# Unit 3 of a fused attention and gated layer kernel: activated in chunks in PSUM and projected by seven products, with the weight sums made two steps earlier

## The chip, the cores and the metric

The kernel runs on one core of a Trainium2 chip. The metric is the device time of one execution in microseconds (us), from repeated runs. All arithmetic is in 32-bit floats.

## The reference

Two stages follow each other. The first is a linear attention with a decaying state, over 4 batches, 8 heads, 768 tokens and a head width of 48:

```python
for t in range(S):
    cur = u * k[t] v[t]^T
    y[t] = r[t] (state + cur)
    state = w[t] * state + k[t] v[t]^T      # w between 0.8 and 0.95
```

The heads of a token are joined to a row of 384 values, which gives 3072 rows `x`. The second stage is a gated layer with 2048 hidden columns:

```python
h = x @ w_in                     # 384 -> 2048
g = h * erf(softplus(h))
out = g @ w_out                  # 2048 -> 384
```

## The kernel before

**Units and steps.** A unit is two batches times 128 tokens, 256 rows in all; there are 12 units, one for each step s of 0 to 11. Step s computes the attention of unit s (`attend` for steps 0 to 4, `attend_late` for 5 to 11) and passes its rows on as `xT`. Beside it, TensorE computes the hidden layer of unit s-1 and the projection of unit s-3. So unit 3 has its hidden layer in step 4, and is projected in step 6. `attend` and `attend_late` issue attention work; between, tokens are worked off that issue pieces of the other two.

**The hidden layer** (`hidden`) comes in 8 pieces (token H). One is 12 TensorE instructions (L775) into one of the two PSUM buffers "m" and a ScalarE copy of 512 columns to SBUF (L784). The buffer is free for the piece after next when that copy is done. Each unit has two halves of hidden columns, g = 0 and 1, each a tile `h` of 8 by 256.

**Activation, two ways.** Where the unit is below `FAST`, `activate` puts three stages on the list `later`, for each half: Softplus of all 2048 columns into the SBUF tile `room` (L757), Erf in place (L760), and two VectorE products h times room (L764). Token A takes stages from that list. From unit `FAST` on, a unit is activated in four chunks of 1024 columns: token s is a Softplus into the first slot of `room` (L731), token e is an Erf from there into a PSUM lane (L735; "ey" into the banks of y, "ep" into the buffer pp1), and token m is VectorE's product of h and that lane (L740). Each change between Softplus and Erf brings a table load on ScalarE.

**Projection, two ways.** `project` (L807) uses 32 products of 128 rows with 384 columns, each of them two TensorE instructions. It comes in 8 pieces (token P); the sixth and the eighth end with a ScalarE copy "o" of 128x384 out of the "m" buffers (L816), and the output is sent. `project_fast` (L883) takes seven block products of 192 columns (the scheme of Strassen and Winograd on 2x2 blocks), 7 pieces of 16 TensorE instructions. For it:

- four sums of weights are formed once, by `mix_weights`: t3, t2 and t4 into the tile `mixed`, and t1 in the place of the upper right block of w_out. This last one destroys a block that `project` needs. Tokens T (VectorE) and G (GpSimd) send one such sum each (L831).
- four sums of activations per unit, S1 to S4, are formed on VectorE by `blend` (L860 to L866), from quarters of h. Tokens k11p, k22y and so on first copy a quarter to a PSUM lane on ScalarE (`to_lane`, L843): the digits name the quarter, the letter the lane (p for pp1, y for the banks of y).

**Order.** All engines run in program order, written out by hand. In steps 0 to 3 the tables STAGES and CONVERT say what goes where; step 3 is `DIRECT - 1`. In step 4 (`DIRECT`) `in_order` does so; from step 5 on the strings LATE and USUAL, seven stages per step ("front", "near", 0 to 4). Token F goes on with `prepare(s + 1)`, which scales r and k for the next step on VectorE (L263), sums products over the heads (L367), with part of the products on GpSimd (L377, L381), and at last forms the tile `own` (L426).

**In `attend_late`,** the order is: products of level 5 (L452), stages front and near, the product kT times spread (L597), stage 0, products of the last level with two copies `own` and one `few` by ScalarE (L471, L557), stage 1, the state products into PSUM (L538), stage 2, the two `middle` adds (L615), stage 3, the new state (L622), stage 4. The next step opens with `from_own(.., 1)` (L486), a small VectorE copy, and level 5 of its own (L452), which waits for the scaling in the last F of the step before.

Of the kernel before, what the change touches and what calls it, by code (L numbers as in the profile page):

```python
# [15 lines left out]
ALU = mybir.AluOpType  # L16

P = 128
FAST = 4
EP = 64  # L20
HC = 64
NC = 2
# [17 lines left out]
DIRECT = 4  # L40
# [21 lines left out]
def kernel(  # L62
# [14 lines left out]
    nc = tc.nc  # L77
    PSUM = bass.MemoryType.PSUM

    n_steps, _, _, JP, C = rkw.shape  # L80
# [4 lines left out]
    _, NT, DM = w_out.shape  # L85
# [45 lines left out]
    def products(shape, n=None):  # L131


        if n is not None:
            return ps_p.tile(shape, FP32, name=f"pp{n}")
        n = 0 if turns["converting"] else turns["next"]
        turns["next"] = 1 - n
        return ps_p.tile(shape, FP32, name=f"pp{n}")
# [31 lines left out]
    def near_log(s):  # L170
        return NEAR_LOG - (s == DIRECT)
# [85 lines left out]
    def scale(s, level):  # L257

        in_t, tots = loaded[s][0], ready[s][1]
        half, nb = 1 << (level - 1), JP * C >> level  # L260
        n = 1 if s > DIRECT and level == LOG else 2
        halves = view(in_t[:, 0:2], half, [[JP * C - half, n], [2 * half, nb], [1, half]])
        nc.vector.tensor_mul(  # L263
            halves, halves, view(tots[level - 1], 0, [[1, n], [2, nb], [0, half]])
        )
# [170 lines left out]
    def parts_of(s):  # L436

        c, i = divmod(s, SPC)
        in_t, vt = loaded[s]
        made, tots, tot = ready[s]  # L440
        ends = tot.rearrange("p (n h) -> p n h", h=NC)
        return c, in_t, vt, made, states[i][c % 2], states[i][1 - c % 2], ends

    def level_products(pp, rk, level):

        half = 1 << (level - 1)
        m = HC if level <= MASKED else half
        for n in range(JP):
            for s0 in range(0, C, HC):
                for e in range(NE):  # L450
                    t0 = s0 if level <= MASKED else s0 + half
                    nc.tensor.matmul(  # L452
                        pp[s0 : s0 + m, e, n, :m],
                        lhsT=rk[rows(e), 1, n, s0 : s0 + m],
                        rhs=rk[rows(e), 0, n, t0 : t0 + m],
                        start=True,
                        stop=True,
                    )
# [166 lines left out]
    def attend(s, xT, place, behind):  # L625

        c, in_t, vt, made, S, S_next, ends = parts_of(s)
        K = in_t[:, 1]
        RK = in_t[:, 0:2]


        following = prepare(s + 1) if s + 1 < n_steps else iter(())
        own = made if s >= DIRECT else att.tile([P, NH, HC], FP32, name="own")

        def keep_busy(*columns):
            zeros = states[1][0][:].rearrange("p n d -> p (n d)")
            for n in columns if not s else ():
                nc.tensor.matmul(
                    y[:].rearrange("p e j q t -> p (e j q t)")[:, :n], lhsT=ident[:],
                    rhs=zeros[:, :n], start=True, stop=True, skip_group_check=True,  # L640
                )

        def stay_warm(times=1, where=None):
            for _ in range(times):
                ps = where or ps_m.tile([P, NP * C], FP32, name="m")
                nc.tensor.matmul(
                    ps[:], lhsT=ident[:], rhs=ws[s][:, :NP], start=True, stop=True
                )

        if s == DIRECT:  # L650
            next(following)
        for level in range(near_log(s) + 1 if s == DIRECT else 1, LOG + 1):
            rk = made[:] if level == 1 else RK
            pp = products([P, NE, JP, HC])
            level_products(pp, rk, level)
            if level == LOG and s == DIRECT:
                spread_blocks(s + 1, pp)
            scale(s, level)
            keep_busy(DM, DM // 2)
            if level == 1 and s == 1:  # L660
                stay_warm()
            if s == 1 and level == 2:
                behind(None)
            got = pp[:].rearrange("p e n t -> p (e n) t")
            if level == 1:
                if not s:
                    nc.vector.tensor_copy(out=first[:], in_=mask_sb[:, 0, :])
                nc.vector.tensor_mul(
                    own[:], got, first[:, None, :].to_broadcast([P, NH, HC])
                )  # L670
            else:
                take_level(own, pp, level)
            if level > 1 and (s, level) != (DIRECT, LOG - 1):
                next(following, None)
            place(level - 1)

        from_own(s, own, 1)
        ps = products([P, JP, P])
        for n in range(JP):
            nc.tensor.transpose(ps[:, n, :], K[:, n, :], ident[:])  # L680
        if not s:
            stay_warm()
        kT = att.tile([P, NH, D], FP32, name="kT", bufs=1)
        nc.scalar.copy(
            kT[:].rearrange("p (e n) d -> p e n d", e=NE),
            ps[:].rearrange("p n (e d) -> p e n d", e=NE)[..., :D],
        )
        if c:
            nc.gpsimd.tensor_mul(
                faded[0][:], S[:], ends[:, :, 0:1].to_broadcast([P, JP, D])  # L690
            )
        next(following, None)
        place(LOG)


        if s:

            ps = products([P, NC, JP, HC], 1 if s == 1 else None)
            ps = [ps[:, h] for h in range(NC)]
        else:  # L700
            ps = [ps_m.tile([P, JP, HC], FP32, name="m") for h in range(NC)]
        state_part(s, kT, ps)
        from_own(s, own, 0)
        if not s:
            stay_warm(1, products([P, NP * C]))
        for e in range(NE):
            if c:
                nc.vector.tensor_add(middle[rows(e)], faded[0][rows(e)], ps[0][rows(e), :, :D])
            else:
                nc.vector.tensor_copy(middle[rows(e)], ps[0][rows(e), :, :D])  # L710
        nc.gpsimd.tensor_mul(faded[1][:], middle[:], ends[:, :, 1:2].to_broadcast([P, JP, D]))
        for e in range(NE):
            nc.vector.tensor_add(S_next[rows(e)], faded[1][rows(e)], ps[1][rows(e), :, :D])
        for _ in following:
            pass
        place(LOG + 1)
        through_state(s, xT)
        behind()
# [23 lines left out]
    def hidden(of, xT, gs, cut):  # L742
# [25 lines left out]
        for g in range(NG):  # L768
            h = hid.tile([P, FG, UNIT], FP32, name="h")
            gs.append(h)  # L770
            for f in range(0, FG, FT):
# [12 lines left out]
                nc.scalar.copy(h[:, f : f + FT, :], ps[:])  # L784
                if of >= FAST:
                    if f % (2 * FT):
# [145 lines left out]
    def piece(kind, of):  # L932
        if not 0 <= of < n_steps:
            return
        if of not in kind:
            if kind is hids:
                kind[of] = hidden(of, xTs[of], gated[of], not of)
            else:
                kind[of] = (project_fast if of >= FAST else project)(of, gated[of])
        next(kind[of])  # L940

    def in_order(s, k):
# [3 lines left out]
        for what in order[k]:  # L946
# [8 lines left out]
    STAGES_LATE = ("front", "near", 0, 1, 2, 3, 4)  # L955
    LATE = {
        DIRECT + 1: (
            "", "", "A P P P A P P", "F F F A P P P", "T", "H H F", "A s H H H F G ep H H H"
        ),
        DIRECT + 2: (  # L960
            "s P", "m", "ey P m s P P ep P m P", "s P P F ey m k22p k11y F F", "S1",
            "S2 S3 H k12p S4 H F", "s H ey m H H F G G s H ep H H",
        ),
        n_steps - 1: (
            "s P", "m", "ey P m s P P ep P", "m P P", "S", "H H", "s H ey m H H s H ep H H"
# [7 lines left out]
    def run_late(s, tokens, following=None):  # L973

        for what in tokens.split():
            if what == "A":
                advance()
            elif what == "P":
                piece(projs, s - 3)
            elif what == "H":  # L980
                piece(hids, s - 1)
            elif what == "F":
                next(following, None)
            elif what in ("T", "G"):
                mixing.send(nc.vector if what == "T" else nc.gpsimd)
            elif what == "s":
                softplus_chunk()
            elif what[0] == "e":
                erf_chunk(what[1])
            elif what == "m":  # L990
                multiply_chunk()
            elif what[0] == "k":
                to_lane(s - 2, what[1:3], what[3])
            else:
                blend(s - 2, *(int(n) for n in what[1:]))
                if what == "S3":
                    del lanes["11"], lanes["22"]
                elif what == "S4":
                    del lanes["12"]
# [15 lines left out]
    mixing = mix_weights()  # L1015
# [6 lines left out]
    with tc.manual_schedule(  # L1022
# [20 lines left out]
        for s in range(n_steps):  # L1043
# [39 lines left out]
            def behind(n=0):  # L1083
                if n is not None:
                    convert_at(LOG + 2)
                    return
                for what in BEHIND_SCALING:
                    conversion.send(what)
# [6 lines left out]
        s = n_steps  # L1095
# [104 lines left out]
```

## Time and profile before

| | |
|---|---|
| median of 3 runs | 604.16 us (604.1 to 604.3) |
| profiled execution | 603.82 us |
| its span, first to last instruction | 602.0 us |
| granted TensorE clock | 1.00 |
| busy: TensorE, VectorE, ScalarE, GpSimd | 588.4, 440.4, 353.5, 289.4 us |
| project, unit 0 to 3: L807 | 256 instructions, mean 491 ns |
| project_fast, unit 4 to 11: L883 | 896 instructions, mean about 330 ns |

The profile comes from one execution, so its sums are made against 603.82, not against the median. Durations of TensorE instructions overlap: what one of them costs in a row of its kind is the distance of its start from the next. Names of lines (L807) are those of the kernel shown above. PE is TensorE, PEld its weight load, DVE VectorE, ACT ScalarE, POOL GpSimd.

### The profile page before, as it was taken

How to read it: one execution, taken by the hardware profiler on the slowest of the kernel's cores; microseconds unless marked ns; L12 is line 12 of the kernel's file. 1: busy time of each engine (PE TensorE's matmuls, PEld its weight loads, DVE VectorE, ACT ScalarE, POOL GpSimd, SP SyncE). 2: the span in 40 equal slices, each digit the busy share in tenths (PEclk: the TensorE clock that was granted, in tenths of full speed). 3: DMA queues.
4: the chain of work that ended last, by engine and by line, in shares of the span. 5: the costliest groups of instructions: out<-in, count | busy, mean ns of one | idle time of the engine just before them, and what ended most of it. 6: DMA issues, size and time to landing. Idle time of an engine off the chain costs nothing.

```text
span 602.0 us, 16529 instructions
## 1 busy us (share of the span) xinstructions
PE 588.4 (98%) x7242; PEld 495.4 (82%) x7242; DVE 440.4 (73%) x508; ACT 353.5 (59%) x461; POOL 289.4 (48%) x298
## 2 busy tenths in 40 slices
PE   8889999999999999899999999999999999999997
PEld 7668787678668758757899899899898898898997
DVE  5688598795995898997899799799799624124140
ACT  2548887626536543466864864765765764756710
POOL 4349275601497579949939639539549100000000
PEclk9999999999999999999999999999999999999999
DMA  8377371541323423334334325333331300000000
GB/s 322 119 281 224 140 267 57 212 142 20 139 71 134 107 73 127 72 116 156 71 104 169 71 105 169 71 106 133 72 106 53 71 9 27 2 20 14 2 26 27
DMA packets 51376, 63.33 MB, mean 105 GB/s; under 512 B 34920, under 2 KB 40296, under 8 KB 49896
## 3 DMA queue, kind: packets, MB, share of 16 engines
q1 hardware_dynamic: 50824, 62.03, 32.0%
q8 instruction: 57, 0.93, 0.6%
q10 hardware_dynamic: 480, 0.25, 0.2%
q14 instruction: 15, 0.12, 0.1%
HBM read 52.39 MB, written 8.69 MB: 101 GB/s over the span
## 4 chain that ended last, share of the span: by engine, by line
PE 70%; DVE 10%; POOL 10%; issue 4%; DMA 4%; ACT 2%; SPq 0%; POOLq 0%; DVEq 0%; ACTq 0%
PE m L775 32%; PE m L883 25%; PE m L807 4%; PE pp L452 4%; POOL words L381 3%; DMA w<-in_rkw 3%; POOL tot_sb L315 2%; DVE in L263 2%; PE y L486 2%; POOL rk L377 2%; POOL words L377 1%; DVE words L381 1%; PE y L512 1%; DVE h L764 1%; PE pp L538 1%
## 5 line engine op out<-in xcount | busy, mean ns | idle before, releaser
L775 PE MATMUL m<-xT,w_in_sb 128*128 128x256 f32 x1152 | 258.4, 382 | 3.1 <-DMA xT<-y 2.4
L775 PEld LDWEIGHTS m<-xT,w_in_sb 128*128 128x128 f32 x1152 | 215.7, 190 | 36.9 <-issue 3.8
L784 ACT COPY h<-m 128x512 f32<-128x512 f32 x96 | 55.8, 581 | 84.9 <-PE m L775 84.7
L263 DVE TENSOR_TENSOR in<-in,tot_sb 128x1024 f32<-128x1024 f32 (+1 forms) x60 | 80.1, 1335 | 23.6 <-PE pp L452 20.8
L807 PE MATMUL m<-w_out_sb,h 128*128 128x384 f32 x256 | 85.8, 491 | 0.0
L381 POOL TENSOR_TENSOR words<-words,rest 128x528 f32<-128x528 f32 (+10 forms) x77 | 80.8, 1050 | 6.0
L377 POOL TENSOR_TENSOR rk<-words 128x528 f32<-128x528 f32 (+3 forms) x28 | 41.5, 1481 | 81.8 <-DVE sums L367 71.4
L807 PEld LDWEIGHTS m<-w_out_sb,h 128*128 128x128 f32 x256 | 47.6, 190 | 31.5
L452 PEld LDWEIGHTS pp<-in 48*64 48x64 f32 (+1 forms) x2368 | 33.8, 125 | 16.3 <-issue 7.8
L315 POOL TENSOR_TENSOR tot_sb<-tot_sb 128x256 f32<-128x256 f32 (+4 forms) x60 | 43.8, 730 | 4.6
L883 PE MATMUL m<-mixed,h 128*128 128x192 f32 x256 | 45.4, 330 | 0.0
L883 PE MATMUL m<-w_out_sb,h 128*128 128x192 f32 x256 | 44.7, 328 | 0.0
L452 PE MATMUL pp<-in 48*64 48x64 f32 (+1 forms) x2368 | 38.4, 212 | 5.2 <-DVE in L263 2.9
L740 DVE TENSOR_TENSOR h<-h,y 128x1024 f32<-128x1024 f32 x16 | 19.5, 1216 | 31.9 <-ACT y L735 31.8
L735 ACT ACT_TABLE_LOAD x32 | 41.1, 1283 | 2.8 <-DVE h L740 1.4
L883 PEld LDWEIGHTS m<-w_out_sb,h 128*128 128x128 f32 x256 | 41.7, 190 | 0.5
L883 PEld LDWEIGHTS m<-mixed,h 128*128 128x128 f32 x256 | 41.4, 190 | 0.7
L731 ACT ACT_TABLE_LOAD x32 | 41.1, 1283 | 0.6
L883 PE MATMUL m<-w_out_sb,room 128*128 128x192 f32 x224 | 38.7, 326 | 0.0
L377 POOL TENSOR_TENSOR words<-words 128x336 f32<-128x336 f32 (+6 forms) x49 | 36.6, 746 | 3.8
L883 PEld LDWEIGHTS m<-w_out_sb,room 128*128 128x128 f32 x224 | 36.8, 190 | 0.0
L367 DVE TENSOR_REDUCE sums<-rk 128x14 f32<-128x672 f32 (+9 forms) x54 | 34.7, 702 | 0.0
(127 smaller groups left out, 821.5 us busy)
## 6 DMA issues: line engine op xcount, KB each, us to landing
in<-in_rkw SPq DMA_DIRECT2D x11, 1024.0 KB, 5.3
words<-in_moe_w_in SPq DMA_DIRECT2D x8, 768.0 KB, 5.7
words<-in_moe_w_out SPq DMA_DIRECT2D x8, 768.0 KB, 5.7
words<-in_rk_rows SPq DMA_DIRECT2D x8, 768.0 KB, 5.3
w<-in_rkw SPq DMA_DIRECT2D x11, 512.0 KB, 6.4
v<-in_v SPq DMA_DIRECT2D x12, 384.0 KB, 5.8
out<-o SPq DMA_DIRECT2D x24, 192.0 KB, 2.6
rest<-in_w_rows SPq DMA_DIRECT2D x8, 384.0 KB, 5.5
```

The lines of the kernel that those rows point to most:

```text
L263: nc.vector.tensor_mul(halves, halves, view(tots[level - 1], 0, [[1, n], [2, nb], [0, half]]))
L315: nc.gpsimd.tensor_mul(new, pair[:, :, 0], pair[:, :, 1])
L367: nc.vector.tensor_reduce(out=view(sums[:], n, [[near * (NEAR + 1), NEAR // near], [NEAR + 1, near - n]]), in_=terms[n], axis=mybir.AxisLi ...
L377: engine.tensor_mul(terms[n], r[:, :, n:], k[:, :, : near - n])
L381: engine.tensor_mul(k[:, :, :m], k[:, :, :m], w[:, :, n : n + m])
L452: nc.tensor.matmul(pp[s0 : s0 + m, e, n, :m], lhsT=rk[rows(e), 1, n, s0 : s0 + m], rhs=rk[rows(e), 0, n, t0 : t0 + m], start=True, stop=True,)
L731: nc.scalar.activation(sp_room, chunks[0], AF.Softplus)
L735: nc.scalar.activation(at, sp_room, AF.Erf)
L775: nc.tensor.matmul(ps[:, ff, :], lhsT=w_in_sb[:, g * FG + f + ff, kk * P : (kk + 1) * P], rhs=xT[:, kk, :], start=kk == 0, stop=kk == KT - 1,)
L784: nc.scalar.copy(h[:, f : f + FT, :], ps[:])
L807: nc.tensor.matmul(ps[j][:], lhsT=gs[g][:, f, j * C : (j + 1) * C], rhs=w_out_sb[:, g * FG + f, :], start=g + f == 0, stop=g == NG - 1 and ...
L883: nc.tensor.matmul(to, lhsT=a[:, f], rhs=b[:, f], start=start and f == 0, stop=f == FG - 1, skip_group_check=True,)
```

## The change

The constant FAST goes from 4 to 3, so that unit 3 too is activated in four chunks and projected by seven products. The three sums t3, t2, t4 are sent to VectorE at the end of step 3 instead of being spread over steps 5 and 6 (VectorE, GpSimd, GpSimd); the fourth, on GpSimd, moves from step 6 to step 5. The string for step 5 is written anew, with all four chunks, the copies and the blends of unit 3 and two chunks of unit 4; step 6 has no string of its own any more and uses USUAL.

```diff
-FAST = 4
+FAST = 3
...
         next(following, None)
         place(LOG)
-
+        if s == DIRECT - 1:
+            for _ in range(3):
+                mixing.send(nc.vector)
...
         DIRECT + 1: (
-            "", "", "A P P P A P P", "F F F A P P P", "T", "H H F", "A s H H H F G ep H H H"
-        ),
-        DIRECT + 2: (
-            "s P", "m", "ey P m s P P ep P m P", "s P P F ey m k22p k11y F F", "S1",
-            "S2 S3 H k12p S4 H F", "s H ey m H H F G G s H ep H H",
+            "", "", "s ey m P s ep m P P s P ey m P", "s P F ep m P k22y F P k11p F", "S1",
+            "S2 S3 H k12y S4 H F", "s H ep m H H F G s H H H ep",
         ),
...
-            elif what in ("T", "G"):
-                mixing.send(nc.vector if what == "T" else nc.gpsimd)
+            elif what == "G":
+                mixing.send(nc.gpsimd)
```

The string that step 6 now uses:

```python
USUAL = (
    "s P", "m", "ey P m s P P ep P", "m k22y P F P k11p F F", "S1", "S2 S3 H k12y S4 H F",
    "s H ey m H H F s H ep H H",
)
```

## The prediction

> **What bounds the kernel now.** The busy table first.
>
> ```profile
> PE 588.4 (98%) x7242; PEld 495.4 (82%) x7242; DVE 440.4 (73%) x508; ACT 353.5 (59%) x461; POOL 289.4 (48%) x298
> ```
>
> TensorE is busy almost throughout, so time changes in two ways only: it gets fewer columns to stream, or its gaps change. Which gaps lie near the change? I cut the PE timeline where `from_own(.., 1)` (L486) opens a step: steps 5, 6 and 7 begin at 202.91, 247.71 and 298.22 us, step 8 at 342.83. Then the busy time by stage (columns: stretch, length, busy time and count by engine):
>
> ```profile
> 202.91:247.71 44.80, 44.80 (x372) 32.78 (x361) 40.35 (x42) 21.60 (x26) 32.56 (x30) 1.00 0.37 113
> 247.71:298.22 50.51, 48.25 (x486) 34.34 (x485) 45.76 (x52) 33.87 (x40) 40.63 (x36) 1.00 0.36 105
> 298.22:342.83 44.61, 44.61 (x533) 40.71 (x532) 40.33 (x50) 29.32 (x37) 31.49 (x42) 1.00 0.38 116
> ```
>
> Step 6 is 5.90 longer than step 7. Both compute a unit's hidden layer and project one unit, but step 6 projects unit 3 by the plain product (L807) and step 7 unit 4 by seven products (L883). PE timeline of step 6, then of step 7:
>
> ```profile
> 247.71 0.66 PE L486 MATMUL y<-own,v 64*48 64x64 f32 x32
> 250.01 1.16 PE L452 MATMUL pp<-in 48*64 48x64 f32 x64 [1.64 <-DVE in L263]
> ...
> 275.62 5.45 PE L775 MATMUL m<-xT,w_in_sb 128*128 128x256 f32 x24
> 281.50 2.86 PE L775 MATMUL m<-xT,w_in_sb 128*128 128x256 f32 x12 [0.43 <-ACT h L784]
> 284.55 13.73 PE L775 MATMUL m<-xT,w_in_sb 128*128 128x256 f32 x60 [0.20 <-ACT h L784]
> ...
> 309.34 2.76 PE L883 MATMUL m<-mixed,room 128*128 128x192 f32 x16
> 311.94 2.76 PE L883 MATMUL m<-w_out_sb,room 128*128 128x192 f32 x16
> ```
>
> The 5.90 split by start times. (a) Projection: its runs take 2.78 + 13.10 + 5.36 = 21.24 in step 6 (64 instructions), 2.79 + 10.60 + 5.40 = 18.79 in step 7 (112): 2.45. (b) Opening: 2.30 against 0.48, because VectorE's scaling L263 is late: 1.82. (c) Hidden layer: 22.60 against 21.00, because ScalarE empties the two "m" buffers late: 1.60. Sum 5.87. Steps 8 and 9 take 44.5 each, so step 7 is the normal length.
>
> [...] The trace has 1283 ns and, for 1024 columns, 1.03 to 1.06 us; it shows no separate drain between load and activation (load 232.88, activation 234.17). [...] The trace agrees (o of L816, ready at 220.6, starts at 222.65 behind an Erf), and my working rests on it. [...] Here two L263 took 3.67 with GpSimd active, one alone 1.23.
>
> **The change, part by part.**
>
> *Unit 3 by seven products (step 6):* -2.45, as (a). The spacing is really below the 190 ns weight load: runs of 16 start 2.60 apart, 0.1625 each.
>
> *Step 6 takes the usual order, with unit 4's second chunk already activated:* it becomes a copy of step 7, and (b) and (c) go. For (b) the cause in step 5 was the two L764 products of unit 3, 5.27 us on VectorE at 243.13, right before the scaling; they are replaced by one 1.21 product. (c) goes as steps 7 to 9 show. -3.42. Two GpSimd sums at 288.0 and 291.4 (3.45 each) become none: GpSimd is earlier, nobody waits for it, 0.
>
> *Three sums on VectorE at the end of step 3.* VectorE and its weight-sum row before:
>
> ```profile
> 146.86 1.14 DVE L708 TENSOR_TENSOR middle<-faded,pp 48x384 f32<-48x384 f32 x2 [5.78 <-PE pp L538]
> ...
> 231.48 2.45 DVE L831 TENSOR_TENSOR mixed<-w_out_sb 128x1536 f32<-128x1536 f32 x1
> ```
>
> VectorE is idle for 5.78 just where the sums are queued, GpSimd too (120 to 148). From 768 columns at 0.95 and 1024 at 1.23, 1536 cost 1.79; three in a chain, 5.5. They fit; at the 2.45 of the row beside GpSimd they would end 1.6 late, and `middle` (done at 148.0) is needed by TensorE at 152.97: 5 us of slack. 0. The last sum stays one GpSimd operation of 3.4 at the same place of step 5. Step 4 loses one Softplus of 2048, off the path: 0.
>
> *Step 5 gets the chunks and blends of unit 3.* ScalarE loses two Erf and one Softplus of 2048 (3.2 each with load); it gains four pairs s, e of 2.35 + 2.34, three lane copies of 1.01, and one more pair of unit 4 (4.7): from 21.6 busy to about 38 in 45. What matters is the order. The start of VectorE's first product is set by this row (VectorE timeline), behind which it stands:
>
> ```profile
> 218.43 1.71 DVE L597 TENSOR_TENSOR kT<-kT,spread 128x768 f32<-128x768 f32 x1
> ```
>
> ScalarE, from 206.23 (its xT transfers issued): s1, e1 into y, s2, e2 into pp, s3, done at 217.95. e3 needs y again, hence product m1, which ends at 221.28. e3 to 223.70; few and own copies (1.35) to 225.0, just before TensorE's L538 needs the bank at 225.93; s4 to 227.3; output copy o of token half 0 (0.48) to 227.74; e4 to 230.1; VectorE's m4 to 231.36; copy k22y to 232.4; **o of half 1**, issued after k22y in the new order, to 232.85; k11p to 233.87; first h copy to 234.4. Before, these two o copies were
>
> ```profile
> 222.65 0.48 ACT L816 COPY o<-m 128x384 f32<-128x384 f32 x1
> 226.03 0.48 ACT L816 COPY o<-m 128x384 f32<-128x384 f32 x1 [2.90 <-PE m L807]
> ```
>
> and freed both "m" buffers before the hidden layer began at 226.79. Now its first piece begins at 227.8 (+1.0), and the second, due at 230.36, waits for the second o to 232.9 (+2.55). Third at 235.5, no wait. VectorE meanwhile: m4, two scalings (3.7) to 235.1, S1 to 236.2; k12y to 237.3; second h copy to 237.8, when the fourth piece is due at 238.0: no wait, by 0.2. Then an activation before the h copies of pieces three and four costs +0.1 and +0.3. Sum +3.95: step 5 takes 48.75. Its other end: VectorE does the row sums by 244.9, the state by 246, m by 247.2, scaling 4 by 248.6, before step 6's products at 252.3, so (b) does not return. SP: output and row loads leave 5 us later, rows landing near 241, needed about 257. 0.
>
> **Sum.** -2.45 - 3.42 (5.90 unrounded) + 3.95 = -1.95. The profiled execution took 603.82 (span 602.0 and 1.8 around it): 601.9. It lies 0.34 under the median 604.16, so 602.2.
>
> Bounds for the unseen cost: the hold-up in step 5 is at least 0 (o copies moved ahead in effect, if ScalarE's chunks run earlier than I place them) and at most what the slower rival gives. I take the worked value; both ends enter the range.
>
> **Rivals.**
>
> *No hold-up in step 5:* if m1 came early enough for e4 to finish before 226, all 5.9 stay: 598.3. Against it: VectorE's timeline has no gap from 205.35 to 220.07, and m1 stands behind all of it. Half a hold-up gives 600.2.
>
> *The blend chain slips (no change):* the fourth piece hangs by 0.2 on scaling, S1, k12y and h copy. With scalings at 2.35 each (seen once, 293.63) and the chain's wake-ups, 1 us slips, plus up to 1 more at e of unit 4: 603.2 to 604.2. GpSimd is active until 241, so this is possible.
>
> *VectorE becomes the bound (slower):* one mechanism: two-input operations run at the shared rate of 2.64 each, as the two L764 at 243.13 did, against 1.2. Place: the scalings and S1 to S3 after m4 at 231.4. Scalings +1.6, S1 +1.4: the fourth piece waits 2.8; S2 and S3 push e of unit 4, behind which the next h copies stand, by 2.0 more: +4.8, 607.0. It turns slower once the slip passes 1.95 + 1.2 = 3.2. Against: S1 to S4 read one operand from PSUM and took 1.21 to 1.22 in step 6 although GpSimd was busy.
>
> *It doesn't do what it says:* if the weight load of 190 ns set the pace, 112 would take 21.3 and not save. The starts at 0.1625 exclude it.
>
> **How the numbers follow.** A measurement of this kernel tells 0.2% (1.2 us) from no change. Forecast (hold-up of 3 to 4.7): 0.55, 601.2 to 603.0. Less hold-up: 0.15, 598.3 to 601. Slip: 0.18, 603.2 to 604.2. Slower: 0.12. Faster 0.66, the same 0.22, slower 0.12, with 0.04 of the forecast inside the band. The range 599.8 to 604.2 leaves out the slower rival and the far end of the first.
>
> **What would show it.** 112 more L883 instructions, 64 fewer L807; L731 and L735 loads 36 each instead of 32; in step 5 TensorE waits of about 1.0 and 2.5 at the first two hidden pieces, behind o of L816; step 5 near 48.7, step 6 near 44.6; no wait at step 6's opening; `through_state` of step 3 on time. Wrong if step 5 stays at 45 or passes 52, if step 6 keeps waits on h, or if step 3 or a step after 7 changes length by over 0.5.

## The result

The changed kernel takes 602.90 us in the median of 18 runs, the kernel before 605.65 beside it: ratio 0.9954, interval 0.9939 to 0.997, that is 2.75 us less (1.8 to 3.7). The forecast was 1.95 less, at 602.2. Both kernels scatter by several us. One cause shows below: part of the executions lose some of TensorE's granted clock, the clock that the chip lets it run at (a mean below 0.998 in 11 of the 18; in the profiled one it is 0.50 for 3.41 us). Among the executions whose mean clock stayed above 0.998, the changed kernel has a median of 601.41 (7 of 18).

The profiled execution took 603.48 with a span of 601.5, only 0.5 under the span before, because it is one of those with a clock loss (mean clock 0.997). Lines from 694 on are two higher in the changed kernel (L775 is now L777, L883 is L885). First the page's busy row:

```profile
PE 585.6 (97%) x7290; PEld 501.7 (83%) x7290; DVE 439.9 (73%) x516; ACT 362.0 (60%) x473; POOL 272.3 (45%) x296
```

It hardly tells anything: TensorE has more instructions and 2.8 us less busy time, ScalarE has 8.5 more. The same stages as before, cut again at `from_own(.., 1)`, tell where the time went. The rows are steps 5, 6 and 7 (stretch, length, busy and count by engine, then the granted clock):

```profile
203.25:253.23 49.98, 46.82 (x371) 33.88 (x361) 41.12 (x48) 35.58 (x41) 31.27 (x38) 0.97 0.34 103
253.23:297.75 44.52, 44.52 (x533) 40.80 (x532) 40.27 (x50) 31.54 (x39) 27.88 (x33) 1.00 0.39 117
297.75:342.28 44.53, 44.53 (x533) 40.80 (x532) 39.94 (x50) 29.32 (x37) 27.85 (x33) 1.00 0.37 117
```

Step 6 fell from 50.51 to 44.52, the length of step 7. Step 5 grew from 44.80 to 49.98, and its clock is 0.97. The steps around them kept their lengths within 0.1; the changed kernel enters step 5 later by 0.34. Inside step 5, on TensorE's timeline:

```profile
226.26 0.94 PE L538 MATMUL pp<-v,kT 64*48 64x48 f32 x64
228.16 2.86 PE L777 MATMUL m<-xT,w_in_sb 128*128 128x256 f32 x12 [0.97 <-ACT o L818]
233.22 20.08 PE L777 MATMUL m<-xT,w_in_sb 128*128 128x256 f32 x84 [2.20 <-ACT o L818]
253.23 0.67 PE L486 MATMUL y<-own,v 64*48 64x64 f32 x32
```

The two waits for the o copies are there, 0.97 and 2.20. The third row has a second loss: from the rate of step 6 (96 instructions in 20.99), 84 need 18.37, and they took 20.08. The clock by stretches explains these 1.71:

```profile
229.98:233.39 3.41, 1.21 (x6) 0.75 (x5) 2.80 (x3) 2.12 (x4) 3.17 (x4) 1.00 0.11 30
233.39:236.80 3.41, 3.41 (x9) 2.70 (x10) 3.36 (x5) 2.23 (x3) 3.03 (x5) 0.50 0.75 250
237.00:253.23 16.23, 16.23 (x77) 14.01 (x75) 12.32 (x19) 10.21 (x12) 9.43 (x16) 1.00 0.45 123
```

Right behind the wait the clock is 0.50 for 3.41 us, then full again. ScalarE's timeline shows why the o copy was late (the same two rows were at 222.65 and 226.03 before):

```profile
227.63 0.48 ACT L818 COPY o<-m 128x384 f32<-128x384 f32 x1
228.13 1.28 ACT L737 ACT_TABLE_LOAD   x1
229.42 1.03 ACT L737 ACTIVATE pp<-room 128x1024 f32<-128x1024 f32 x1
231.74 1.02 ACT L845 COPY y<-h 128x1024 f32<-128x1024 f32 x1 [1.29 <-DVE h L742]
232.69 0.47 ACT L818 COPY o<-m 128x384 f32<-128x384 f32 x1
```

The second o, whose products were finished near 226, stands behind k22y (L845), which itself waits 1.29 for VectorE's product m of the fourth chunk (L742).

### The profile page after: what moved, and what is told of

It is laid out like the page before. It is cut to its first block, busy times and chain, and to the rows that moved or that the text cites. A ratio compares the mean times of both kernels' runs of the same rounds, so it can differ in the third digit from the quotient of the medians.

```text
span 601.5 us, 16645 instructions
## 1 busy us (share of the span) xinstructions
PE 585.6 (97%) x7290; PEld 501.7 (83%) x7290; DVE 439.9 (73%) x516; ACT 362.0 (60%) x473; POOL 272.3 (45%) x296
## 4 chain that ended last, share of the span: by engine, by line
PE 81%; DVE 8%; DMA 4%; ACT 3%; issue 2%; POOL 2%; SPq 0%; POOLq 0%; DVEq 0%; ACTq 0%
PE m L777 38%; PE m L885 28%; PE m L809 4%; PE pp L452 4%; DMA w<-in_rkw 3%; PE y L486 2%; PE y L512 1%; DVE in L263 1%; PE pp L538 1%; DVE sums L367 1%; DVE words L381 1%; DVE rk L377 1%; POOL tot_sb L315 1%; POOL w_in_sb L232 1%; DVE own L464 1%
## 5 line engine op out<-in xcount | busy, mean ns | idle before, releaser
L777 PE MATMUL m<-xT,w_in_sb 128*128 128x256 f32 x1152 | 259.3, 383 | 5.7 <-ACT o L818 3.2
L777 PEld LDWEIGHTS m<-xT,w_in_sb 128*128 128x128 f32 x1152 | 217.2, 191 | 38.9 <-issue 3.8
L786 ACT COPY h<-m 128x512 f32<-128x512 f32 x96 | 55.8, 582 | 85.8 <-PE m L777 85.7
L809 PE MATMUL m<-w_out_sb,h 128*128 128x384 f32 x192 | 64.3, 491 | 0.0
L809 PEld LDWEIGHTS m<-w_out_sb,h 128*128 128x128 f32 x192 | 35.7, 190 | 23.6
L885 PE MATMUL m<-mixed,h 128*128 128x192 f32 x288 | 51.1, 331 | 0.0
L885 PE MATMUL m<-w_out_sb,h 128*128 128x192 f32 x288 | 50.3, 329 | 0.0
L885 PEld LDWEIGHTS m<-w_out_sb,h 128*128 128x128 f32 x288 | 46.9, 190 | 0.5
L885 PEld LDWEIGHTS m<-mixed,h 128*128 128x128 f32 x288 | 46.6, 190 | 0.9
L885 PE MATMUL m<-w_out_sb,room 128*128 128x192 f32 x256 | 44.2, 326 | 0.0
L315 POOL TENSOR_TENSOR tot_sb<-tot_sb 128x256 f32<-128x256 f32 (+4 forms) x60 | 40.4, 673 | 4.5
L742 DVE TENSOR_TENSOR h<-h,y 128x1024 f32<-128x1024 f32 x17 | 20.7, 1215 | 29.6 <-ACT y L737 29.5
L885 PEld LDWEIGHTS m<-w_out_sb,room 128*128 128x128 f32 x256 | 42.0, 190 | 0.0
L733 ACT ACTIVATE room<-h 128x1024 f32<-128x1024 f32 x36 | 38.1, 1057 | 0.4
L742 DVE TENSOR_TENSOR h<-h,pp 128x1024 f32<-128x1024 f32 x19 | 23.0, 1212 | 20.8 <-ACT pp L737 20.8
```

The source lines that it names most:

```text
L315: nc.gpsimd.tensor_mul(new, pair[:, :, 0], pair[:, :, 1])
L733: nc.scalar.activation(sp_room, chunks[0], AF.Softplus)
L742: nc.vector.tensor_mul(h, h, at)
L777: nc.tensor.matmul(ps[:, ff, :], lhsT=w_in_sb[:, g * FG + f + ff, kk * P : (kk + 1) * P], rhs=xT[:, kk, :], start=kk == 0, stop=kk == KT - 1,)
L809: nc.tensor.matmul(ps[j][:], lhsT=gs[g][:, f, j * C : (j + 1) * C], rhs=w_out_sb[:, g * FG + f, :], start=g + f == 0, stop=g == NG - 1 and ...
L885: nc.tensor.matmul(to, lhsT=a[:, f], rhs=b[:, f], start=start and f == 0, stop=f == FG - 1, skip_group_check=True,)
```

## The experiments

**The second o copy ahead of k22y.**

```diff
-"s P F ep m P k22y F P k11p F"
+"s P F ep m P P k22y F k11p F"
```

> The changed kernel, with the eighth projection piece of step 5 (and with it the second o copy) issued ahead of k22y; nothing else moves. Theory A (the second wait of step 5 is the o copy standing behind k22y, which stands behind the product m4): the o copy comes at about 230.9 instead of 232.7, the second hidden piece waits about 0.3 instead of 2.2; k22y, k11p and the first h copy come about 0.3 later than this piece needs, so pieces 3 and 4 wait 0.7 and 0.3. Idle before the hidden layer of step 5: about 2.3 instead of 3.2, no single wait above 1. With full clock throughout: 1 us less than the changed kernel at full clock. Theory B (the half clock of 3.4 us in step 5 of the changed kernel's profile comes from the wait of 2.2 there): it is gone in nearly all executions, another 1 us less in the median, so 2 less in all, near 600.9. Rival (half clock comes at any place, whatever the waits): as often as in the changed kernel, median only 1 less. Rival to A (the wait is set by the first o or by the state products): time as the changed kernel's.

Measured 601.36 (0.9938 of before, 0.9917 to 0.9959), 600.77 at full clock (3 of 6). In step 5 TensorE's timeline has these rows:

```profile
227.73 5.60 PE L777 MATMUL m<-xT,w_in_sb 128*128 128x256 f32 x24 [0.96 <-ACT o L818]
233.84 16.69 PE L777 MATMUL m<-xT,w_in_sb 128*128 128x256 f32 x72 [0.50 <-ACT h L786]
```

The wait of 2.20 is gone: the o copy came at 229.96. But the gain at full clock (mean clock above 0.998, here and below) is 0.6, not 1. In the place of the o copy, the h copies are late (TensorE's weight loads waited for L786 four times, 2.2 in all), so the step takes 47.64, where 44.80 was its length before the change. Most of the wait had only moved on in ScalarE's queue, to the copies behind k22y. On half clock it says little: theory B expected it to be gone in nearly all executions, and 3 of 6 are below 0.998.

**The first product m ahead of the row sums.**

```diff
-"", "", "s ey m P s ep m P P s P ey m P", "s P F ep m P k22y F P k11p F",
+"s", "ey m s", "ep P P s ey P m P P m", "s P F ep P P m k22y F k11p F",
```

> The changed kernel, with another string for step 5: front s, near ey m s, stage 0 'ep P P s ey P m P P m', stage 1 's P F ep P P m k22y F k11p F'. So the first product m stands ahead of the row sums and of kT times spread, and both o copies ahead of k22y. Theory A (the whole hold-up is a chain that begins with m1 standing behind kT times spread): m1 at about 214 instead of 220.4, e3 no longer waits, both o copies done by 227.8, k22y at 228.7; no wait above 0.3 in step 5, which takes 45 us as before the change, about 3.2 (waits) less than the changed kernel at full clock. Theory B (half clock follows the wait): no half clock in step 5, median 4 to 5 under the changed kernel's, 598 to 599. Rival (half clock at any place): median 3 less, with the same scatter. Rival (VectorE is the bound: m1 moved ahead delays row sums, GpSimd's terms and the scaling by 1.2): a new wait of 1 to 2 at the opening of step 6, gain only 1 to 2.

Measured 598.41 (0.9893, 0.9874 to 0.9913), 598.26 at full clock (4 of 6): the fastest kernel of all, 6.1 under before. VectorE's timeline, with the product (L742) now ahead of the row sums (L367) and L597; in the changed kernel it stood behind them. First that kernel's row, then the two of this run:

```profile
220.41 1.21 DVE L742 TENSOR_TENSOR h<-h,y 128x1024 f32<-128x1024 f32 x1
```

```profile
214.98 1.21 DVE L742 TENSOR_TENSOR h<-h,y 128x1024 f32<-128x1024 f32 x1
216.11 2.37 DVE L367 TENSOR_REDUCE sums<-rk 128x15 f32<-128x720 f32 x3
```

and the stages of steps 5 and 6:

```profile
204.25:249.04 44.79, 44.79 (x370) 32.78 (x360) 41.15 (x48) 35.55 (x41) 31.27 (x32) 1.00 0.38 115
249.04:293.57 44.53, 44.53 (x533) 40.79 (x533) 40.49 (x50) 31.53 (x39) 29.77 (x40) 1.00 0.39 116
```

Step 5 is back to 44.79 although ScalarE is as busy as in the changed kernel (35.55 and 35.58). So ScalarE's load was not the cost: its order was. The rival (a new wait at the opening of step 6) is refuted. The edit does two things, though: it also puts both o copies ahead of k22y, which alone brought 0.6 (the run above). The early product without that was not run. In this trace k22y ends at 230.13, so an o copy behind it would end near 230.6, just before the second piece is due at 230.75; that is an estimate. The half clock of this profile (mean 0.997) lies in the first 20 us (mean clock 0.92 there, 1.00 in every later stretch), not here.

**The sums alone.** To the kernel before, only the sums' places:

```diff
+        if s == DIRECT - 1:
+            for _ in range(3):
+                mixing.send(nc.vector)
...
-"F F F A P P P", "T", "H H F", "A s H H H F G ep H H H"
+"F F F A P P P", "", "H H F", "A s H H H F ep H H H"
...
-"s H ey m H H F G G s H ep H H"
+"s H ey m H H F G s H ep H H"
```

> The kernel before (unit 3 by the plain product), with only the weight sums moved: t3, t2, t4 on VectorE at the end of step 3, the fourth sum on GpSimd in step 6, none in step 5. Theory (sums fit into VectorE's idle 5.78 of step 3; the opening wait of step 6 comes from the two products L764 of 5.27 in step 5): step 3 unchanged within 0.1, the wait of 1.64 at the opening of step 6 stays above 1, time within 0.2% of before. Rival (the wait came from the sums T and G in step 5, which slowed L764 through GpSimd): L764 takes about 2.6 instead of 5.27, the wait is gone, 1.6 to 2 less than before. Rival (the sums delay middle in step 3): through_state waits, up to 2 more.

Measured 602.12 (0.9955, 0.9943 to 0.9968), 601.90 at full clock, 2.3 under before. My theory fell, and of the rivals the first holds. VectorE's timeline in step 5, before and then with the sums moved (L764 is L766 there, and L765 in the next run):

```profile
243.13 5.27 DVE L764 TENSOR_TENSOR h<-h,room 128x1024 f32<-128x1024 f32 x2
```

```profile
241.19 2.78 DVE L766 TENSOR_TENSOR h<-h,room 128x1024 f32<-128x1024 f32 x2
243.89 1.42 DVE L263 TENSOR_TENSOR in<-in,tot_sb 128x1024 f32<-128x1024 f32 x1
```

The two products that I had named as the cause take 2.78 where they stood at 5.27, and the opening of step 6 has no wait (247.12 to 247.60). Part of the wait on h in step 6 went too (0.43 is left of 0.43 and 0.20). In ratio to before, this brings what the whole change brings: 0.9955 and 0.9954. It isn't quite the change's own part on the sums, though: here no sum is left in step 5, while the change keeps the fourth there, on GpSimd.

**Which sum?** Two kernels, each with one sum of step 5 taken away. T made in step 3, the GpSimd sum left:

```diff
+        if s == DIRECT - 1:
+            mixing.send(nc.vector)
...
-"F F F A P P P", "T", "H H F",
+"F F F A P P P", "", "H H F",
```

> The kernel before, with one of the four sums moved: t3 on VectorE at the end of step 3; the GpSimd sum of step 5 and the two of step 6 stay. It splits what the three sums moved together brought (2.4 in the run of the sums alone). Theory C (the opening wait of step 6 came from the GpSimd sum beside the two products L764[...]): L764 stays near 5.2, the wait stays at 1.2 to 1.7, time within 0.5 of before. Rival (it came from VectorE's own queue, 2.45 shorter without t3): the row sums L367 wait for GpSimd until 240 all the same, but L764 begins earlier and the wait falls below 0.5, time 1.5 less.

and T left in step 5, the GpSimd sum moved to step 6:

```diff
-"A s H H H F G ep H H H"
+"A s H H H F ep H H H"
...
-"s H ey m H H F G G s H ep H H"
+"s H ey m H H F G G G s H ep H H"
```

> The kernel before, with the GpSimd sum of step 5 moved behind: step 6 makes three sums on GpSimd, t3 stays on VectorE in step 5. Theory C (GpSimd sum beside L764): the two products take near 2.8 instead of 5.27, the opening wait of step 6 goes, about 1.8 less than before (some of it lost if three sums at the end of step 6 slow VectorE there). Rival (VectorE's own queue): wait and time as before.

Measured 602.87 (0.9963, 0.9948 to 0.9977) and 603.52 (0.998, 0.9967 to 0.9993). Without T, VectorE and then TensorE:

```profile
242.12 5.28 DVE L765 TENSOR_TENSOR h<-h,room 128x1024 f32<-128x1024 f32 x2
```

```profile
249.01 1.16 PE L452 MATMUL pp<-in 48*64 48x64 f32 x64 [0.23 <-DVE in L263]
```

With the GpSimd sum late, VectorE:

```profile
243.01 2.78 DVE L764 TENSOR_TENSOR h<-h,room 128x1024 f32<-128x1024 f32 x2
```

Each theory is half right. With the GpSimd sum in step 5 the two products take 2.5 longer (5.28 or 2.78), as theory C says, and without it the opening of step 6 has no wait. But without T everything on VectorE comes 1.4 earlier (state add at 240.97 instead of 241.99, with a start of the step that is 0.4 later), and that alone cuts the wait from 1.64 to 0.23. So the lateness of 1.8 takes both sums: with the GpSimd sum alone 0.4 of it is left, with the VectorE sum alone nothing. The three GpSimd sums at the end of step 6 cost something there: its second wait on h grew from 0.20 to 0.60, and step 7 takes 45.53 instead of 44.61, so the gain is smaller.

**The sums at the front of step 5 on GpSimd.** The changed kernel, with its three lines in step 3 taken out and

```diff
-"", "", "s ey m P s ep
+"G G G", "", "s ey m P s ep
```

> The changed kernel without its step 3 part: t3, t2, t4 on GpSimd at the front of step 5, where GpSimd is idle for 10 us, the fourth as in the changed kernel. Theory (their place in step 3 costs nothing, and beside VectorE's two-input products L377, L381 of step 5 they would): the row of products from 206 to 214 gets 2 to 5 longer, m1 and all behind it later by as much, the waits at the hidden layer of step 5 grow by as much: 2 to 5 above the changed kernel (and half clock more often). Rival (GpSimd's idle stretch hides them): as the changed kernel, within 0.5.

Measured 609.86 (1.0069, 1.0046 to 1.0092): 7 above the changed kernel, more than the 2 to 5 expected. The sums started earlier than I had placed them, at 195.57, as GpSimd had run ahead, and met other products of VectorE than I had said (lines numbered as in the kernel before):

```profile
200.00 4.46 DVE L426 TENSOR_TENSOR own<-block_sb,by_tokens 128x1024 f32<-128x1024 f32 x1
204.39 6.43 DVE L764 TENSOR_TENSOR h<-h,room 128x1024 f32<-128x1024 f32 x2
```

In the changed kernel these are 1.37 and 2.65. The first product m comes at 227.72, 7.3 later, and TensorE waits 6.88 at L538 and 1.34 at the hidden layer, 8.2 instead of 3.2. The clock is 0.92 from 221.0 to 232.5 and 0.60 from 232.6 to 242.8, and the 96 instructions of the hidden layer take 23.61, where step 6 has 20.99. So the place in step 3 is worth much against this one, and a late m1 is a way in which this change could have been a loss.

**A longer wait, twice.** The o copy one place later, and then with k11p made twice in front of it:

```diff
-"s P F ep m P k22y F P k11p F"
+"s P F ep m P k22y F k11p P F"
```

> The changed kernel, with the eighth projection piece of step 5 one place later, behind k11p and the scaling that follows it: the dose the other way. Theory A: the second o copy comes 0.95 later, at 233.7, the second hidden piece waits 3.1 instead of 2.2; step 5 gets 1 longer. Theory B (half clock follows the length of the wait): half clock in most or all executions, 1.7 each: median 1.5 to 2.5 above the changed kernel's. Rival (half clock has nothing to do with the wait): 1 more, scatter as in the changed kernel. Rival to A (something else sets the second wait): no change.

```diff
-"s P F ep m P k22y F P k11p F"
+"s P F ep m P k22y F k11p k11p P F"
```

> The kernel with the second o copy of step 5 one place later, and the copy k11p in front of it made twice (the second writes the same values again): a wait of 4.1 at the second hidden piece. Theory B (half clock follows a long wait, more often the longer it is): clock below 0.998 in nearly every execution; fastest executions 1 above the kernel with a wait of 3.1, so about 603.5 where the clock stays full and 605.3 where it doesn't, median about 605.5 to 606.5. Rival (no relation to the wait): half clock as often as in the kernel before (about a third), median 1 above 603.5 at most.

Measured 605.27 (0.9999, 0.9986 to 1.0012) and 606.33 (1.0015, 1.0002 to 1.0028). TensorE's row of the second hidden piece and what follows, first of the one, then of the other:

```profile
235.25 19.94 PE L777 MATMUL m<-xT,w_in_sb 128*128 128x256 f32 x84 [3.14 <-ACT o L818]
```

```profile
234.72 21.05 PE L777 MATMUL m<-xT,w_in_sb 128*128 128x256 f32 x84 [4.19 <-ACT o L818]
```

The waits are 3.14 and 4.19 as worked out (3.1 and 4.1), and the 84 instructions lose 1.6 and 2.7 to the clock. Executions with a mean clock below 0.998:

| longest wait of step 5 or of step 6's opening | kernels | executions |
|---|---|---|
| up to 1.0 us | o ahead, early m, sums alone, t3 alone, g late | 22 of 68 |
| 1.64 | before, beside the first and the second four | 13 of 37; 33 of 61 |
| 2.20 | changed | 11 of 18 |
| 3.14 | o later | 19 of 22 |
| 4.19 | o latest | 22 of 22 |
| 6.88 | sums in step 5 | 6 of 6 |

From 3.14 on nearly all executions have it, which the rival (no relation) doesn't give. At 1.64 and 2.20 the shares don't separate: the kernel before alone has 13 of 37 beside one set of runs and 33 of 61 beside the other. The executions without a long wait have it in a third; where, a mean clock can't tell. The one such profile at hand (early m) has it in the first 20 us (mean clock 0.92).

## Why the prediction was right, and where it was off

**The projection, -2.45: right.** Step 6's three runs of L885 take 2.79 + 10.60 + 5.40, as step 7's did.

**Step 6 a copy of step 7, -3.42: right in sum, wrong in cause.** Step 6 takes 44.52. But the step that said "the cause in step 5 was the two L764 products" failed: 2.5 of their 5.27 came with the GpSimd sum, and the VectorE sum pushed the same chain back by 1.4. The three sums were booked at 0 in step 3, which holds (1.74 to 1.76 each, 1.79 forecast; they end at 146.75 and `middle` starts at 147.22, waiting for TensorE). What I left out is what their absence does in step 5: with no sum left there the time falls by 2.3 at full clock, with only T gone by 1.5, and the whole change brings 2.7. That the number of this term came out all the same is luck: the change also takes the two products away. By their length (5.27 against 1.22) that would have been enough for the opening of step 6, but no run took them away and left the sums; the two gains overlap and don't add.

**Step 5, +3.95: mechanism right, size slightly high.** The working took ScalarE's instructions in the order in which they were issued, and the runs show it for the second o copy: in the changed kernel, issued behind k22y, it started at 232.69 and k22y at 231.74; in the first experiment, issued ahead of it, it started at 229.96 and k22y at 231.31. The step began 0.34 later than the forecast had it. Shifted by that, m1 should have ended at 221.62 and the o copies at 228.08 and 233.19; they ended at 221.62, 228.11 and 233.16. The hold-ups of 1.0 and 2.55, reckoned from start to start, came to 1.04 and 2.44 (0.97 and 2.20 in the profile's rows count from the modelled end of the instruction before). The term that was too large is +0.1 and +0.3 at later pieces: the profile has no wait there, though the half clock of this execution (0.50 from 233.39 to 236.80) also gave ScalarE more time just then. VectorE's two scalings took 2.85, not 3.7. Without the clock loss the step takes 49.98 - 1.71 = 48.27, +3.47.

**Not foreseen: the half clock.** My sum priced a wait at its length. In the profiled execution the half clock behind the wait of 2.20 cost 1.71 more. At full clock the change is worth about 2.7 (601.41 against 604.1 to 604.2 for before, in other runs), and as the kernel before has half-clock executions as well, the medians differ by nearly the same. That the term left out cancels in the difference is luck too.

**The rivals.** No hold-up would have been 598.3 by my working; the early product gives 598.41. Among the slower kernels, the one with GpSimd sums in step 5 does what the slower rival said (VectorE slowed beside GpSimd: 6.43 instead of 2.65 for two products), at another place in the queue.

## What to carry to other kernels

A copy that frees the buffer of the bound engine should not stand in a queue behind an instruction that waits for a third engine: find the first wait of such a chain (here one VectorE product behind seven others) and move that, since moving the last link alone mostly shifted the wait (0.6 less at full clock; with the early product 3.15 less). Work on a side engine that was "free" can come with longer instructions on its neighbour (two products took 5.28 beside a GpSimd sum of 3.44, and 2.78 with the sum moved); book what its removal gives, not only what its new place costs. A gap on TensorE can cost more than its own length: the 84 instructions behind the wait of 2.20, with 3.41 us at a clock of 0.50, took 1.71 longer than at full clock, those behind the wait of 4.19 took 2.7 longer.

## What the runs showed of the hardware

**The clock behind a wait.** A wait of 2.20 was followed by a TensorE clock of 0.50 for 3.41 us (the changed kernel, the row 233.39:236.80 above). Around one of 3.14 (o later) the clock was 0.97 from 232.1 to 235.2, 0.50 from 235.2 to 238.4 and 1.00 from 239. Around one of 4.19 (o latest) it was 0.83 from 230.5 to 234.7, so it fell while TensorE still waited, and 0.60 from 234.8 to 241.5. If it was always either 1.00 or 0.50, these two rows give about 6.8 us at half clock, and the two rows of the 6.88 (sums in step 5) about 10.0: estimates from the means.

A wait of 1.64 was not followed by half clock in the profile of the kernel before. This stretch holds 1.54 of the 1.64, and from its end to 253.30 the clock is 1.00 as well:

```profile
246.50:249.91 3.41, 1.87 (x38) 1.29 (x37) 3.41 (x3) 2.07 (x3) 3.25 (x3) 1.00 0.70 103
```

So in these five profiles a longer wait never came with less time at half clock. Why executions of one kernel differ (11 of 18 of the changed kernel are below 0.998) was not shown: of most only the mean clock is kept.

**VectorE's products with both operands in SBUF, beside GpSimd.** The GpSimd sum of step 5, in the kernel before:

```profile
241.91 3.43 POOL L831 TENSOR_TENSOR mixed<-mixed,w_out_sb 128x1536 f32<-128x1536 f32 x1
```

It ends at 245.34. Of the two L764 products (243.13 to 248.41), the first took 3.29 and the second 2.06. The GpSimd operation behind the sum (L315, from 245.30) took 2.02; with the sum moved to step 6 it took 1.04. The GpSimd sums in step 5 show the same on both engines: `own` took 4.46 instead of 1.37, and the second and the third sum took 4.30 and 4.29 where the first had taken 3.44. The "shared rate of 2.64" of the prediction is only half of the 5.27 that these two unequal products took. With the sum moved, the two met shorter GpSimd operations (128x256) and took 2.78 together. A product with one operand in PSUM (L740 at 292.49), wholly inside a GpSimd sum, took its usual 1.22. What makes the one kind longer and not the other was not shown.
